# A new order of steps in batch 0 of a fused attention and feed-forward kernel, with its strided V loaded head by head

## The chip, the cores and the metric

The kernel runs on one core of a Trainium2 chip. The metric is the device time of one execution in microseconds (us); a kernel is given by the median of its runs. A core has five engines with instruction queues of their own: TensorE (PE, matmuls and the loads of their weights), VectorE (DVE), ScalarE (ACT), GpSimd (POOL) and SyncE (SP). An engine takes its queue in order, and waits on semaphores for what others make. POOL and SP also issue DMA transfers. PE writes its results to PSUM, which has eight banks; DVE and ACT read them there.

## The reference

Sparse attention over 8 batches and 8 heads of 576 positions with 64 elements each, then a feed-forward layer over all 4608 tokens:

```python
scores = scale * np.matmul(q, k.transpose(0, 1, 3, 2))
rel = pos[:, None] - pos[None, :]
mask_local = (rel >= 0) & (rel < stride)                       # heads 0 to 3, stride = 32
mask_strided = (rel >= 0) & (pos[None, :] % stride == pos[:, None] % stride)   # heads 4 to 7
scores = np.where(masks, scores, -1e9); attn = softmax(scores)
x = (attn @ v).transpose(0, 2, 1, 3).reshape(B * S, H * D)
out = (relu(x @ w_in) ** 2) @ w_out                            # 512 -> 2048 -> 512
```

## The kernel before

The feed-forward layer is done in nine chunks of 512 tokens: for each, 16 × 4 matmuls on w_in (`mm1`, line 856; `ff` is one of the 16 blocks of 128 hidden columns, `kk` one of the four blocks of 128 input rows), Relu on ACT (862), the square on DVE (866), and 16 × 4 matmuls on w_out (`mm2`, 962). The last two chunks take another way (932). The attention of batches 1 to 7 is woven between these matmuls by `PLAN`, which names for each group of four matmuls the steps that go ahead of it. Batch 0 has nothing to hide behind, since the first chunk needs its result; its steps stand in the string `BATCH0`, one word a step, and are issued in that order by `run_step`. All engines get their instructions in the order in which the steps issue them. So the order of the words is the order of the queues.

A unit is a pair of heads. Units 0 and 1 of batch 0 are local heads (0 to 3), units 2 and 3 strided ones (4 to 7). The words, with the PSUM bank that a step writes behind the slash (a step that takes a pair of banks takes this one and the next):

- `c1kv`: cast unit 1's k on the engine given by the last letter (a is ACT, v is DVE, g is POOL), line 303. `T1kv/0`: six transposes of it on PE (492) into bank 0, and a copy from there by DVE (499) into kTl; for q into qT.
- `W0k1v/5`: the same for the strided heads: transposes of half 1 of batch 0's strided k (337), and a copy (342) into kT_s; for q into qT_s. The source is staged in parts of w_out's tile, loaded by line 314.
- `b3.0/2`: the mask bias of unit 3, half 0: one matmul of the identity with a stored bias into each bank of the pair 2 and 3 (514), which starts the sums there.
- `S3.0`: the scores of unit 3, half 0, added onto that bias (544), and their exp on ACT (548). Where no `b` has gone before, `S` writes the bias itself and its word carries the bank.
- `N3/2`: sums of the exps by matmuls with ones (768), then Ln and Exp on ACT (770, 772), for a strided unit. `O3/2`: its product with V (782), and the division by the sums on DVE (784) into xt, the input of the feed-forward layer.
- `D0/4`: the product of a local unit's exps with V, which carries a column of ones (797), reciprocal and product on DVE (803, 804) into x_l. `E0v/4`: six transposes of that (837) and a copy (840) into xt.
- `H0v`: V of the local heads, shifted by 32 rows, on DVE (450). `z`: the mask of the later batches, on DVE (1067, 1068). `w1/7`: one matmul on a cleared tile (979), with no use but to keep PE at work.
- `P01/5`: the four partial sums of the first chunk's `ff` 1 begin with `kk` 0, in bank 5. Sixteen such words, for `ff` 0 to 3, end the string.

The loads that batch 0 and the first chunk need are issued ahead of the string by `load_v0` and its neighbours: q and k of unit 0 on SP, and on POOL, in this order, strided q, strided k (`load_str_rows`, 314), unit 1's q and k (296), V of the local heads (443), V of the strided heads (757), and w_in in four pieces (455). The first two pieces hold `ff` 0 to 3 (`kk` 0 and 2, then 1 and 3), the third `ff` 4 to 9, the fourth the rest. V of the strided heads goes to a part of the first chunk's tile g_sb that is free until then. It is cast from 32 to 16 bits under way, as all loads on POOL are.

Of the kernel before, what the change touches and what calls it, by code (L numbers as in the profile page):

```python
# [14 lines left out]

NP = 4
BATCH0 = """
    c0qa c0kv T0qa/2 w1/7 T0kv/5 S0.1/0 W0q0v/3 S0.0/4 W0q1v/2 b3.1/6 z W0k0a/1 W0k1v/5 b3.0/2 c1kv w1/0 S3.1
    b2.1/4 S3.0 c1qv T1kv/0 H0v S2.1 b2.0/6 S2.0 N3/2 T1qv/1 D0/4 b1.0/6 S1.0 b1.1/0 O3/2 S1.1 E0v/4 N2/6 D1/0
    P01/5 P02/3 O2/6 P03/2 P00/4 P30 P31 P32 P33 E1a/1 P20 P21 P22 P23 P10 P11 P12 P13  # L20
"""
PLAN = """
# [117 lines left out]
def kernel(  # L140
# [9 lines left out]
    nc = tc.nc  # L150
# [8 lines left out]
    NJ = 8  # L159
# [96 lines left out]
    b0 = g_pool.tile([128, 16, 512], BF16, name="g_sb").rearrange("p a c -> p (a c)")  # L256
    n_s = 4 * NJ * D
    vs0 = b0[0:SP_, 0:n_s].rearrange("p (u n d) -> p u n d", u=2, d=D)
# [181 lines left out]
    def load_v_local_sw(b):  # L440
        i = (2 * b) % NV
        t = vl_all[:, i:i + 2]
        nc.gpsimd.dma_start(out=t[32:128, :, :, :, 0:D].rearrange("p u h t d -> p (u h t) d"),  # L443
                            in_=v[b, 0:4].rearrange("h (t p) d -> p (h t) d", p=QL))
        for u in range(2):
            st.setdefault(4 * b + u, {})["v"] = t[:, u]
# [307 lines left out]

    def load_v0():
        load_v_local_sw(0)
        nc.gpsimd.dma_start(
            out=vs0.rearrange("p u n d -> p (u n d)").rearrange("p (h c) -> p h c", h=4),
            in_=v[0, 4:8].rearrange("h (p j) d -> p h (j d)", j=NJ))

    def step_N(u):
        e, hw = st[u]["e"], S // 2
# [354 lines left out]
    for i in range(2):  # L1117
# [8 lines left out]
                            NEG, -NEG, op0=ALU.mult, op1=ALU.add)  # L1126
    load_qk_local_sw(0, (1,))
    load_v0()
    for i in range(4):
        load_w_in(i)  # L1130
# [35 lines left out]
    for line in PLAN.strip().splitlines():  # L1166
        n, words = line.split(":")
# [42 lines left out]
```

## Time and profile before

| | us |
|---|---|
| median of 3 runs | 295.37 |
| lowest, highest | 295.08, 299.47 |
| the profiled execution: its time | 295.08 |
| the profiled execution: span of the core | 293.4 |

The span runs from the first instruction to the last in the profile; the profiled execution's time holds 1.7 us more around it. The mean granted clock of TensorE in it was 0.998 of full speed. Rows of groups and timelines give a start and a length in us, the engine, the line of the kernel, what is written and read, how many instructions, and in brackets the idle time of the engine ahead of them with what ended it. The chain of waits follows the last instruction back to what released it, step by step. Matmuls are pipelined: a row's length holds the time until the last result is out, and the next group begins before that, so the pace of PE is read from one start to the next. In answers by stretch the numbers are the length, then busy time and count for PE, weight loads, DVE, ACT and POOL, the granted clock, the share of the DMA engines and GB/s.

### The profile page before, as it was taken

What the parts mean: (1) busy time and instruction counts of PE and PEld (TensorE: products, weight loads), DVE (VectorE), ACT (ScalarE), POOL (GpSimd) and SP (SyncE); (2) the same over time, 40 slices, a digit from 0 to 9 for tenths busy, and PEclk for the clock granted to TensorE, in tenths of its full rate; (3) what the DMA queues carried; (4) which work ended last, traced back from release to release, by engine and by line L of the source; (5) the groups of instructions that cost most, each with busy time, mean ns of one, the idle gap of its engine ahead of it and who ended that gap; (6) DMA issues with size and microseconds to landing.
All of it is one profiled execution on the core that took longest, in us unless ns stands there. A gap on an engine that the chain in (4) does not pass through costs nothing.

```text
span 293.4 us, 6453 instructions
## 1 busy us (share of the span) xinstructions
PE 287.2 (98%) x2506; PEld 152.5 (52%) x2506; DVE 199.9 (68%) x489; ACT 167.0 (57%) x306; POOL 86.7 (30%) x135
## 2 busy tenths in 40 slices
PE   7999999999999999999999999999999999999995
PEld 3554555544444454544445444444444444984594
DVE  5666797776366746866366826673389979968983
ACT  3767846674657644764567446654676367306610
POOL 8974552062343047074303720000000013102300
PEclk9999999999999999999999999999999999999999
DMA  7999999999999999999998997411001200020003
GB/s 151 180 210 207 199 201 181 171 246 107 185 218 165 129 190 212 152 135 179 179 141 115 178 169 147 84 56 74 36 22 38 93 36 0 2 107 37 2 1 143
DMA packets 91470, 37.23 MB, mean 127 GB/s; under 512 B 77668, under 2 KB 84226, under 8 KB 91440
## 3 DMA queue, kind: packets, MB, share of 16 engines
q0 software_dynamic: 50352, 18.14, 55.6%
q1 hardware_dynamic: 40944, 18.62, 31.2%
q8 instruction: 19, 0.31, 0.4%
q14 instruction: 11, 0.09, 0.1%
q10 hardware_dynamic: 144, 0.07, 0.1%
HBM read 36.83 MB, written 9.44 MB: 158 GB/s over the span
## 4 chain that ended last, share of the span: by engine, by line
PE 96%; DMA 2%; DVE 0%; issue 0%; DVEq 0%; POOLq 0%
PE psb L856 43%; PE psb L962 33%; PE psb L932 9%; DMA w_out_b<-in_q_dram 2%; PE psb L815 2%; PE psb L589 1%; PE psb L544 1%; PE psb L492 1%; PE psb L743 1%; PE psb L680 1%; PE psb L748 1%; PE psb L514 1%; PE psb L337 0%; PE psb L837 0%; PE psb L327 0%
## 5 line engine op out<-in xcount | busy, mean ns | idle before, releaser
L856 PE MATMUL psb<-xt,w_in 128*128 128x512 bf16 x576 | 131.6, 379 | 0.0
L862 ACT ACTIVATE r<-psb 128x512 bf16<-128x512 f32 x144 | 85.6, 599 | 45.6 <-PE psb L856 42.5
L962 PE MATMUL psb<-w_out_b,g_sb 128*128 128x512 bf16 x448 | 101.0, 379 | 0.0
L856 PEld LDWEIGHTS <-w_in 128*128 128x128 bf16 x576 | 53.8, 98 | 60.3 <-issue 0.5
L866 DVE TENSOR_TENSOR g_sb<-r 128x512 bf16<-128x512 bf16 x112 | 47.0, 423 | 43.8 <-ACT r L862 42.6
L962 PEld LDWEIGHTS <-g_sb 128*128 128x128 bf16 x448 | 42.0, 98 | 47.6
L966 ACT COPY y<-psb 128x512 f32<-128x512 f32 x28 | 16.5, 589 | 42.6 <-PE psb L962 42.5
L901 POOL CAST sa<-g_sb 128x256 fp32r<-128x256 bf16 x16 | 9.7, 603 | 98.1 <-DVE g_sb L896 98.1
L725 DVE TENSOR_TENSOR xt<-psb,rv 64x288 bf16<-64x288 f32 x36 | 17.3, 479 | 14.3 <-ACT rv L713 13.9
L599 ACT ACTIVATE e<-psb 128x384 bf16<-128x384 f32 x36 | 15.5, 505 | 2.8 <-PE psb L589 2.8
L821 DVE TENSOR_TENSOR x_l<-psb,rinv 96x384 bf16<-96x384 f32 x28 | 15.5, 554 | 1.0
L596 DVE TENSOR_TENSOR e<-e,mask_all 128x576 bf16<-128x576 bf16 x24 | 10.0, 454 | 8.8 <-ACT e L599 8.6
L896 DVE TENSOR_TENSOR g_sb<-r 128x512 bf16<-128x512 bf16 x32 | 13.0, 419 | 3.3 <-ACT r L862 3.3
L355 POOL DMA_DIRECT2D q_t<-in_q_dram x6 | 3.4, 568 | 38.0 <-DMA qT_s<-q_t 35.9
L284 POOL DMA_DIRECT2D q_l<-in_q_dram x16 | 11.6, 729 | 8.1 <-DMA v_s<-in_v_dram 3.7
L284 POOL DMA_DIRECT2D k_l<-in_k_dram x16 | 11.7, 735 | 1.7 <-issue 0.9
L932 PE MATMUL psb<-t,s 128*128 128x256 f32 x96 | 12.2, 283 | 0.0
L718 DVE TENSOR_TENSOR xt<-psb,rv 64x162 bf16<-64x162 f32 x24 | 11.2, 469 | 1.2 <-ACT rv L713 0.5
L932 PEld LDWEIGHTS psb<-t,s 128*128 128x128 f32 x96 | 11.6, 189 | 0.0
L355 POOL DMA_DIRECT2D k_t<-in_k_dram x6 | 3.2, 536 | 27.3 <-DMA kT_s<-k_t 25.9
L944 DVE TENSOR_TENSOR y<-psb,y 128x256 f32<-128x256 f32 x19 | 8.0, 423 | 4.3 <-PE psb L932 3.5
L443 POOL DMA_DIRECT2D vl<-in_v_dram x8 | 9.8, 1226 | 3.8 <-DVE xt L718 2.9
(153 smaller groups left out, 303.4 us busy)
## 6 DMA issues: line engine op xcount, KB each, us to landing
out_dram<-y SPq DMA_DIRECT2D x35, 256.0 KB, 2.7
vl<-in_v_dram POOLq DMA_DIRECT2D x8, 288.0 KB, 8.2
w_out_b<-in_moe_w_out_dram POOLq DMA_DIRECT2D x4, 512.0 KB, 14.7
q_t<-in_q_dram POOLq DMA_DIRECT2D x7, 288.0 KB, 6.3
k_t<-in_k_dram POOLq DMA_DIRECT2D x7, 288.0 KB, 7.2
w_in<-in_moe_w_in_dram POOLq DMA_DIRECT2D x2, 768.0 KB, 13.5
v_s<-in_v_dram POOLq DMA_DIRECT2D x12, 108.0 KB, 7.7
k_l<-in_k_dram POOLq DMA_DIRECT2D x16, 72.0 KB, 7.5
```

Source lines behind the costliest of these rows:

```text
L284: nc.gpsimd.dma_start(out=t[:, :, hh, :], in_=src[b, 2 * p + hh].rearrange("(t p) d -> p t d", p=QL))
L599: nc.scalar.activation(e[:, row, 4 * QL * i:4 * QL * (i + 1)], bk[row][i][:, 0:4 * QL], AF.Exp, scale=scale)
L718: nc.vector.tensor_tensor(t, po[half(par), f].rearrange("c (a g m) -> c g m a", a=n, g=3), rv[half(par), w * f:w * (f + 1)].rearrange("c ( ...
L725: nc.vector.tensor_tensor(to[:, :, :, :, par], po[half(par)].rearrange("c f (a h m) -> c h m f a", a=n, h=3)[:, h], rv[half(par)].rearrang ...
L821: nc.vector.tensor_tensor(x, po[0:QL, :, 0:D], rinv[0:QL].to_broadcast([QL, NL, D]), op=ALU.mult)
L856: nc.tensor.matmul(ph, w_in_tile(kk, ff), xt[kk][:, 512 * c:512 * (c + 1)], start=(kk == order[0]), stop=(kk == order[-1]))
L862: nc.scalar.activation(r, ph, AF.Relu)
L866: later(1, lambda: nc.vector.tensor_tensor(g[:, ff, :], r, r, op=ALU.mult))
L896: nc.vector.tensor_tensor(g[:, ff, :], r, r, op=ALU.mult)
L932: nc.tensor.matmul(pa, a, b, start=k == 0 and n not in "273", stop=k == 7, skip_group_check=True)
L962: nc.tensor.matmul(py, g[:, ff, 128 * j:128 * (j + 1)], w_out_b[:, ff, :], start=(ff == 0), stop=(ff == 15))
L966: nc.scalar.copy(y, py)
```

## The change

The words of `BATCH0` are put into another order, with other banks, and one warm-up word (`w1/0`) is left out. No step is added. The biases b0.1 (which `S0.1` wrote itself) and b2.0 come before the first scores, b2.1 and b3.1 where their banks allow, `z` goes between the two copies of strided q, T1q before S2.0 and ahead of H0v, b1.0 ahead of D0, S1.0 and S1.1 ahead of O3. V of the strided heads is loaded by four transfers of 72 partitions × 512 elements instead of one of 72 × 4 × 512.

```diff
 BATCH0 = """
-    c0qa c0kv T0qa/2 w1/7 T0kv/5 S0.1/0 W0q0v/3 S0.0/4 W0q1v/2 b3.1/6 z W0k0a/1 W0k1v/5 b3.0/2 c1kv w1/0 S3.1
-    b2.1/4 S3.0 c1qv T1kv/0 H0v S2.1 b2.0/6 S2.0 N3/2 T1qv/1 D0/4 b1.0/6 S1.0 b1.1/0 O3/2 S1.1 E0v/4 N2/6 D1/0
+    c0qa c0kv T0qa/2 w1/7 T0kv/5 b0.1/0 b2.0/6 S0.1 W0q0v/3 z S0.0/4 W0q1v/2 b3.1/0 W0k0a/3 W0k1v/2 b2.1/4 S3.1
+    c1kv b3.0/2 S3.0 c1qv T1kv/0 S2.1 T1qv/1 H0v S2.0 N3/2 b1.0/6 D0/4 S1.0 b1.1/0 S1.1 O3/2 E0v/4 N2/6 D1/0
     P01/5 P02/3 O2/6 P03/2 P00/4 P30 P31 P32 P33 E1a/1 P20 P21 P22 P23 P10 P11 P12 P13
 """
...
     def load_v0():
         load_v_local_sw(0)
-        nc.gpsimd.dma_start(
-            out=vs0.rearrange("p u n d -> p (u n d)").rearrange("p (h c) -> p h c", h=4),
-            in_=v[0, 4:8].rearrange("h (p j) d -> p h (j d)", j=NJ))
+        to = vs0.rearrange("p u n d -> p (u n d)").rearrange("p (h c) -> p h c", h=4)
+        for h in range(4):
+            nc.gpsimd.dma_start(out=to[:, h], in_=v[0, 4 + h].rearrange("(p j) d -> p (j d)", j=NJ))
```

In the built program the queues of ACT and SP are in the same order as before. On PE two instructions fewer stand (the warm-up matmul and its weight load), on POOL three transfers more. The transfers that POOL issues take eight semaphores in turn, before and after.

## Prediction

> **What bounds the kernel now.** I read the page first: its busy times and the shares of the chain of work that ended last.
>
> ```profile
> PE 287.2 (98%) x2506; PEld 152.5 (52%) x2506; DVE 199.9 (68%) x489; ACT 167.0 (57%) x306; POOL 86.7 (30%) x135
> PE 96%; DMA 2%; DVE 0%; issue 0%; DVEq 0%; POOLq 0%
> ```
>
> TensorE (PE) carries the end. Second, the windows by stage (PE's share is the first number after the comma) say where it still has holes.
>
> ```profile
> 5.20:10.40 5.20, 4.21 (x61) 2.77 (x60) 2.86 (x7) 2.58 (x4) 5.20 (x7) 1.00 1.43 174
> 10.40:16.80 6.40, 6.03 (x118) 4.05 (x119) 5.36 (x10) 5.35 (x9) 6.03 (x8) 1.00 1.40 194
> 16.80:21.10 4.30, 4.30 (x45) 2.00 (x41) 1.85 (x3) 2.16 (x5) 2.99 (x4) 1.00 1.15 209
> 21.10:50.00 28.90, 28.90 (x270) 15.58 (x270) 22.29 (x59) 20.20 (x42) 13.02 (x23) 1.00 1.28 199
> ```
>
> From 16.8 to 50 us PE has no hole, and the chain leaves PE hardly room for one later, so the change, which lies wholly before 21 us, can only shift the start of that dense stretch. Even if every hole between 5.2 and 16.8 us went, 0.99 + 0.37 = 1.4 us would be won, 0.5% of the span. Two things can set the start of the dense stretch: PE's own chain through batch 0, and the third piece of w_in, which ff 4 needs. The timelines of PE and of its weight loads show both (start, length, line, what ended an idle time).
>
> ```profile
> 7.12 0.30 PE L544 MATMUL psb<-qT,kTl 64*128 64x96 bf16 x6 [0.61 <-DVE kTl L499]
> 7.79 0.43 PE L337 MATMUL psb<-ident,w_out_b 96*128 96x96 bf16 x6 [0.37 <-DMA w_out_b<-in_q_dram]
> 9.22 0.68 PE L337 MATMUL psb<-ident,w_out_b 96*128 96x96 bf16 x12
> 9.99 0.38 PE L979 MATMUL psb<-xt 128*128 128x512 bf16 x1
> 10.38 0.56 PE L544 MATMUL psb<-qT_s,kT_s 64*72 64x72 bf16 x8
> 11.49 0.43 PE L492 MATMUL psb<-ident,k_l 96*128 96x96 bf16 x6
> 11.85 0.33 PE L544 MATMUL psb<-qT_s,kT_s 64*72 64x72 bf16 x8
> 12.11 0.44 PE L514 MATMUL psb<-w_out_b,ident 72*72 72x288 bf16 x2
> 12.48 0.33 PE L544 MATMUL psb<-qT_s,kT_s 64*72 64x72 bf16 x8
> 13.10 0.43 PE L492 MATMUL psb<-ident,q_l 96*128 96x96 bf16 x6
> 13.37 0.53 PE L797 MATMUL psb<-vl,e 128*128 128x65 bf16 x12
> 14.45 0.30 PE L544 MATMUL psb<-qT,kTl 64*128 64x96 bf16 x6 [0.31 <-DVE qT L499]
> 15.65 0.43 PE L837 MATMUL psb<-ident,x_l 96*128 96x96 bf16 x6
> 16.83 0.59 PE L856 MATMUL psb<-xt,w_in 128*128 128x512 bf16 x2
> 21.11 4.86 PEld L856 LDWEIGHTS <-w_in 128*128 128x128 bf16 x24 [0.39 <-DMA w_in<-in_moe_w_in_dram]
> ```
>
> The last row is the second gate: PE's queue of weight loads reaches ff 4 and finds w_in not there. The loads beside it (issue times in POOL's timeline; KB and time from issue to landing in the answers on the DMA issues):
>
> ```profile
> 5.81 1.18 POOL L443 DMA_DIRECT2D vl<-in_v_dram  x1
> 6.98 0.75 POOL L757 DMA_DIRECT2D g_sb<-in_v_dram  x1
> 7.73 2.93 POOL L455 DMA_DIRECT2D w_in<-in_moe_w_in_dram  x4
> 13.28 0.56 POOL L318 DMA_DIRECT2D q_t<-in_q_dram  x1 [0.29 <-POOL q_t L1085]
> 25.13 0.55 POOL L430 DMA_DIRECT2D v_st<-in_v_dram  x1 [2.81 <-DMA w_in<-in_moe_w_in_dram]
> g_sb<-in_v_dram POOLq DMA_DIRECT2D x1, 288.0 KB, 7.5
> w_in<-in_moe_w_in_dram POOLq DMA_DIRECT2D x1, 256.0 KB, 8.0
> w_in<-in_moe_w_in_dram POOLq DMA_DIRECT2D x1, 768.0 KB, 11.9
> vl<-in_v_dram POOLq DMA_DIRECT2D x1, 288.0 KB, 6.8
> ```
>
> They land at 5.81 + 6.8 = 12.6 (V of the local heads), 6.98 + 7.5 = 14.5 (strided V), 7.73 + 8.0 = 15.7 (first piece of w_in) and 9.19 + 11.9 = 21.1 us (third piece). The first piece, issued 0.75 us after the strided V, lands 1.2 us after it though each takes 7.5 to 8 us: the loads queue behind each other, and the queue, not the issue, sets when they land. So PE's chain and w_in meet at 21.1 us almost exactly, and a gain needs both.
>
> **The change part by part.** *Biases ahead.* b2.0 (a two-matmul bias of scores, 12.11 to 12.48 = 0.37 us of PE) goes into the hole of 0.61 us that ended at 7.12; that hole waits for DVE's kTl copy, so it costs nothing there and takes 0.37 us out of the later stretch. b0.1 only stands before S0.1 as it did. The warm-up matmul at 9.99 goes: it stood where PE waits for ACT's kT_s copy, which ends 10.33, so nothing is won. *z moves up* between the two qT_s copies, and the rows of DVE and ACT for this and what follows are:
>
> ```profile
> 9.18 0.46 DVE L342 COPY qT_s<-psb 128x576 bf16<-128x576 bf16 x1 [0.46 <-PE psb L337]
> 9.55 0.50 DVE L1067 COPY mask_all<-mask_loc 128x576 bf16<-128x576 bf16 x1
> 10.16 0.46 DVE L342 COPY kT_s<-psb 128x576 bf16<-128x576 bf16 x1
> 11.96 0.76 DVE L499 COPY kTl<-psb 128x576 bf16<-128x576 bf16 x1 [0.45 <-PE psb L492]
> 12.75 0.58 DVE L450 COPY vl<-vl 32x1280 bf16<-32x1280 bf16 x1
> 13.64 0.76 DVE L499 COPY qT<-psb 128x576 bf16<-128x576 bf16 x1 [0.31 <-PE psb L492]
> 14.31 0.22 DVE L803 RECIPROCAL rinv<-psb 96x12 f32<-96x12 f32 x1
> 14.57 0.95 DVE L804 TENSOR_TENSOR x_l<-psb,rinv 96x768 bf16<-96x768 f32 x1
> 9.69 0.64 ACT L342 COPY kT_s<-psb 128x576 bf16<-128x576 bf16 x1 [0.29 <-PE psb L337]
> 10.98 2.51 ACT L548 ACTIVATE e<-psb 72x576 bf16<-72x576 f32 x4 [0.65 <-PE psb L544]
> ```
>
> z takes 9.55 to 10.16, 0.61 us; the idle time that it now falls into is 0.46 us and copies overlap by some 0.08, so the second qT_s copy ends about 9.72 instead of 9.64. *Banks.* W0k1 now writes bank 2, which that copy reads: it starts about 9.77, not at 9.22 + 0.68/2, some 9.5. DVE's kT_s copy, which waited for z, now waits for PE: 10.25 to 10.71 against 10.62. S3.1 starts at 10.4 as before and ends 0.08 later, at 11.02. Its exp on ACT (2.51/4 = 0.63 us each) runs 11.06 to 11.70.
>
> T1k now writes bank 0, which S3.1's scores hold until that exp has read them. By PE's own pace it would start at 11.57; it waits until 11.75, 0.26 later than the 11.49 of before. The kTl copy on DVE follows, 12.22 to 12.98 (0.76). *T1q ahead of S2.0.* T1q starts 0.26 after S2.1, at 12.37; its copy, which in the trace held S1.0 until 14.45, now runs right behind the other, to about 13.7, and S1.0 waits for it no more. What is late next: behind it on DVE stands H0v (0.58 us), which before went first. It ends about 14.25, and all of D0 but its first matmul needs the shifted V: D0 runs from 14.3 instead of 13.37. *b1.0 ahead of D0.* It writes banks 6 and 7, where S2.0's scores stand until its exp has ended: S2.0 is on PE at 12.73 to 13.06, its exp at 13.10 to 13.75, so b1.0 starts at 13.80, with D0 queued behind it; by this alone D0 would start at 14.05. Both waits lie in the same place, and H0v's ends last.
>
> From D0 the way to the dense stretch is fixed: D0's 0.5 us to 14.8, reciprocal 0.2 and x_l 0.95 to 16.1, E0 at 16.1 instead of 15.65 (+0.45). The bias, S1.0, S1.1 and O3 fit before it. E0, N2 and D1 keep their 16.83 − 15.65 = 1.18 us at most, so the first matmul on w_in is at some 17.25, +0.4. From there to ff 4 PE needs 4.2 us (4.28 in the trace, with the last 0.1 a wait for w_in, which now is in time): 21.45 against 21.11. Taken: **+0.3 us**. Bounds: if H0v ends earlier than I put it and only b1.0's wait is left, D0 at 14.05 gives +0.1; if each of the three new hand-overs (bank 2, bank 0, banks 6 and 7) costs 0.1 more, +0.6. Below nothing, too: were none of them waited for, PE would save the 0.37 of the bias and the 0.45 between S1.0's own pace (14.0) and 14.45, and the gate would be w_in. I take the value near the upper half because each wait follows from rows with less than 0.2 us of slack.
>
> *V by heads.* One issue of 0.75 us becomes four. No 72-partition issue of one head is in the trace; the nearest rows are 0.56 us (q_t, 72 partitions) and 0.75 (the load replaced), so POOL is later by 4 × 0.56 − 0.75 = 1.5 to 4 × 0.75 − 0.75 = 2.25 us. Behind stand w_in, the rest of batch 0 and 1 and w_out. The third piece of w_in would be issued at 10.7 to 11.4; the DMA queue reaches it only after the pieces before it, which land from 15.7 on. Cost nothing while that backlog of 4 us or more lasts; without it, up to 2.25 us. Each load on POOL also waits for the one eight before it (the row at 25.13: the 18th load waits for w_in's last piece, the 10th). The fourth piece of w_in thus comes to wait for the local V, landed at 12.6, instead of going out at 9.9; again before the queue gets to it. O3 needs the last V head at 15.4; the whole V landed at 14.5. Cost 0.
>
> [...]
>
> Sum: 295.08 (the profiled execution; span 293.4) + 0.3 = 295.4. The median of the runs shown, 295.37, is 0.29 above it, and that is the base of the forecast: 295.37 + 0.3 = **295.7 us**.
>
> **The rivals.** [...]
>
> *No change.* The bias taken away and the waits added cancel, and w_in still lands at 21.1: 295.4.
>
> *Slower: w_in late.* If the four V loads run one behind another, each with its own time in the queue (14.5 − 12.6 = 1.9 us for the whole V), w_in lands 3 × 1.9 = 5.7 us later, at 26.8, and the dense stretch with it: 301. It costs from the point where w_in passes 21.45, and passes 2% at 21.11 + 5.9 = 27.0. With only half of it, 298. Against: the backlog above.
>
> **How the numbers follow.** Forecast (+0.1 to +0.6) 0.55; faster 0.2; no change 0.17; slower by w_in 0.08, a quarter of it beyond 2%. 2% is 5.9 us, about what a measurement of this kernel can tell from no change; even the whole hole of 1.4 us stays within it. Hence faster 0.01, same 0.97, slower 0.02. The range runs from the lower end of the faster rival, 294.5, to the forecast's upper bound with 0.5 of the late-w_in case, 295.37 + 0.6 + 0.5 = 296.5; the likeliest case by itself is 295.4 to 296.0.
>
> **What would show it.** In the changed profile: two strided biases before 7.1 us; T1k (L492 on k_l) at 11.75 behind an ACT wait; H0v (L450) after both L499 copies and D0 (L797) ending at 14.8; E0 (L837) at 16.1, the first L856 at 17.2 to 17.3, and ff 4 at 21.4 to 21.5 with no wait for w_in. Four V issues of 0.5 to 0.75 us on POOL, w_in 1.5 to 2.3 us later issued and no later landed. Wrong if D0 starts before 14.0, or if the weight loads of ff 4 again end a wait for w_in.

## The result and the profile after

| | before | the whole change |
|---|---|---|
| runs | 22 | 22 |
| median, us | 295.18 | 296.37 |
| lowest, highest | 294.54, 299.47 | 295.15, 301.71 |
| runs at or above 298 us | 1 | 10 |
| median of the other runs | 295.16 | 295.56 |
| the profiled execution, its span | 295.08, 293.4 | 295.50, 293.8 |

The kernel became slower: the ratio after to before is 1.0058 [1.0034, 1.0081], some 1.7 us, and stays within 2%. A ratio, here and below, leaves out the runs more than 1.5% above the fastest of the same kernel (of the changed kernel those at 301.42 and 301.71 us), so where long runs are many, as in some experiments, it understates them and the counts say more.

The runs of the changed kernel fall into two groups with nothing between them. Twelve lie from 295.15 to 296.39 us, and the mean granted clock of TensorE in them was 0.992 to 1.000. Ten lie from 298.22 to 301.71, with a clock of 0.972 to 0.988. The profiled execution is of the first group. So there are two things to explain: 0.4 us between the lower groups (295.56 − 295.16), and 3 to 6 us, which some executions pay and others do not. The first is not steady: measured again twice (e5_again and f16_again below), it was 0.20 and 0.02 us.

What this execution pays for the order can be read in the profile after. First the page's busy times: PE has the warm-up matmul less, POOL the three transfers more.

```profile
PE 284.4 (97%) x2469; PEld 152.7 (52%) x2505; DVE 199.6 (68%) x489; ACT 167.0 (57%) x306; POOL 87.6 (30%) x138
```

Then the windows by stage, with the same columns as in the prediction.

```profile
5.20:10.40 5.20, 4.13 (x60) 2.64 (x58) 2.55 (x7) 2.58 (x4) 4.55 (x8) 1.00 1.24 159
10.40:16.80 6.40, 5.58 (x107) 3.83 (x108) 4.80 (x10) 4.99 (x8) 4.82 (x7) 1.00 1.44 190
16.80:21.10 4.30, 4.15 (x49) 2.27 (x50) 2.09 (x4) 2.21 (x4) 4.20 (x5) 1.00 1.15 207
21.10:50.00 28.90, 28.63 (x265) 15.46 (x269) 21.71 (x58) 20.27 (x41) 13.70 (x25) 1.00 1.29 201
```

PE's holes between 5.2 and 16.8 us have grown from 0.99 + 0.37 = 1.36 us to 1.07 + 0.82 = 1.89. The second row holds most of it. The timelines of PE, of its weight loads and of DVE show the steps that the prediction named:

```profile
6.92 0.30 PE L544 MATMUL psb<-qT,kTl 64*128 64x96 bf16 x6 [0.36 <-DVE kTl L499]
9.27 0.70 PE L337 MATMUL psb<-ident,w_out_b 96*128 96x96 bf16 x12
10.43 0.35 PE L544 MATMUL psb<-qT_s,kT_s 64*72 64x72 bf16 x8 [0.21 <-ACT kT_s L342]
11.52 0.41 PE L492 MATMUL psb<-ident,k_l 96*128 96x96 bf16 x6
12.13 0.43 PE L492 MATMUL psb<-ident,q_l 96*128 96x96 bf16 x6
13.55 0.41 PE L514 MATMUL psb<-w_out_b,ident 128*128 128x288 bf16 x2 [0.37 <-ACT e L548]
13.80 0.81 PE L797 MATMUL psb<-vl,e 128*128 128x65 bf16 x12
15.99 0.43 PE L837 MATMUL psb<-ident,x_l 96*128 96x96 bf16 x6 [0.18 <-DVE x_l L804]
17.09 0.38 PE L856 MATMUL psb<-xt,w_in 128*128 128x512 bf16 x1
21.39 0.55 PEld L856 LDWEIGHTS <-w_in 128*128 128x128 bf16 x4 [0.41 <-DMA w_in<-in_moe_w_in_dram]
12.72 0.75 DVE L499 COPY qT<-psb 128x576 bf16<-128x576 bf16 x1
13.50 0.57 DVE L450 COPY vl<-vl 32x1280 bf16<-32x1280 bf16 x1
```

H0v (L450) now stands behind both kTl and qT and ends at 14.07, so D0 (L797), which began with 0.53 us at 13.37, takes 0.81 from 13.80. E0 (L837) is 0.34 us later, the first matmul on w_in 0.26, the weight loads of ff 4 0.28. That is the 0.3 to 0.4 us of this execution. In the profiles of e5_again and f16_again the first matmul on w_in came as late (17.12 and 17.16), but the weight loads of ff 4 did not wait for w_in and came at 21.12 and 21.17, against 21.11 before. POOL's issues and the DMA answer:

```profile
6.72 2.20 POOL L759 DMA_DIRECT2D g_sb<-in_v_dram  x4
9.51 2.28 POOL L455 DMA_DIRECT2D w_in<-in_moe_w_in_dram  x3 [0.59 <-DMA w_out_b<-in_k_dram]
13.03 0.74 POOL L455 DMA_DIRECT2D w_in<-in_moe_w_in_dram  x1 [1.24 <-DMA vl<-in_v_dram]
w_in<-in_moe_w_in_dram POOLq DMA_DIRECT2D x1, 768.0 KB, 10.3
```

The issues of w_in begin 1.8 us later (9.51 against 7.73), but its third piece, issued at 11.0, takes 10.3 us where it took 11.9, and lands at 21.3 against 21.1 (at 20.9 in another profiled execution of the same kernel, e5_again below). Nothing in this profile explains the second group, since its clock was full. That needed the experiments.

### The profile page after: what moved, and what is told of

The parts are those of the page before. It is cut to its first block, busy times and chain, and to the rows that moved or that the text cites. A ratio compares the mean times of both kernels' runs of the same rounds, so it can differ in the third digit from the quotient of the medians.

```text
span 293.8 us, 6417 instructions
## 1 busy us (share of the span) xinstructions
PE 284.4 (97%) x2469; PEld 152.7 (52%) x2505; DVE 199.6 (68%) x489; ACT 167.0 (57%) x306; POOL 87.6 (30%) x138
## 4 chain that ended last, share of the span: by engine, by line
PE 88%; DVE 5%; DMA 2%; issue 2%; ACT 1%; POOL 0%; DVEq 0%; POOLq 0%
PE psb L856 38%; PE psb L962 33%; PE psb L932 9%; DMA w_out_b<-in_k_dram 2%; DVE g_sb L896 2%; PE psb L815 2%; PE psb L589 1%; DVE s L903 1%; DVE s L902 1%; PE psb L492 1%; PE psb L743 1%; PE psb L680 1%; PE psb L748 1%; PE psb L544 0%; PE psb L837 0%
## 5 line engine op out<-in xcount | busy, mean ns | idle before, releaser
L856 PE MATMUL psb<-xt,w_in 128*128 128x512 bf16 x556 | 130.1, 379 | 1.0
L962 PE MATMUL psb<-w_out_b,g_sb 128*128 128x512 bf16 x432 | 99.0, 379 | 1.4 <-issue 0.8
L856 PEld LDWEIGHTS <-w_in 128*128 128x128 bf16 x576 | 53.8, 98 | 60.3 <-DMA w_in<-in_moe_w_in_dram 0.4
L725 DVE TENSOR_TENSOR xt<-psb,rv 64x288 bf16<-64x288 f32 x36 | 17.2, 479 | 14.5 <-ACT rv L713 14.0
L718 DVE TENSOR_TENSOR xt<-psb,rv 64x162 bf16<-64x162 f32 x24 | 11.2, 467 | 1.2 <-ACT rv L713 0.5
L815 PEld LDWEIGHTS <-e 128*128 128x128 bf16 x168 | 8.2, 98 | 5.0
## 6 DMA issues: line engine op xcount, KB each, us to landing
w_in<-in_moe_w_in_dram POOLq DMA_DIRECT2D x2, 768.0 KB, 11.2
```

The source lines that it names most:

```text
L725: nc.vector.tensor_tensor(to[:, :, :, :, par], po[half(par)].rearrange("c f (a h m) -> c h m f a", a=n, h=3)[:, h], rv[half(par)].rearrang ...
L815: nc.tensor.matmul(po[:, n, :], e[:, c:c + 128], rhs[:, NL * part + n, 0:D + 1], start=True, stop=True)
L856: nc.tensor.matmul(ph, w_in_tile(kk, ff), xt[kk][:, 512 * c:512 * (c + 1)], start=(kk == order[0]), stop=(kk == order[-1]))
L962: nc.tensor.matmul(py, g[:, ff, 128 * j:128 * (j + 1)], w_out_b[:, ff, :], start=(ff == 0), stop=(ff == 15))
```

## The experiments

Three theories. **Path**: the change costs what PE's chain and w_in show, up to 0.4 us, and the rest is chance. **Clock**: the new order leaves PE emptier in batch 0, and in some executions TensorE's granted clock falls back there (0.50 in the profiles of e2_order and f14_order below). **Heads**: the four V loads cause it, by what they do to POOL and the DMA queue. In the diffs below, only the words of `BATCH0` that change and their neighbours are shown; the first line says against which kernel. The numbers are collected in this table. "High" counts the runs at or above 298 us, "long fall" those of them with a mean clock of 0.989 or less. One stretch of 3.41 us at half clock (e6_fill's profile below has one, the four others with a fall three or four) takes 0.6% off the mean of a span of 293 us, to 0.994, so a long fall is, by its mean clock, two such stretches or more. Of the 22 runs above, all ten high ones are long falls, but elsewhere seven high runs of variants lie at 0.993 or 0.994, and three, of e8_h0 and f15_d0_first, at 0.998 to 1.000: those three are long for another reason than the clock, and the 1.7 us (3.41 / 2) that one stretch costs at most is not all of what the seven pay. "Low median" is that of the runs below 298 us, with before's beside it.

| kernel | runs | high | long fall | low median, us (before) | ratio to before [95%] | before beside it: runs, high |
|---|---|---|---|---|---|---|
| whole change | 22 | 10 | 10 | 295.56 (295.16) | 1.0058 [1.0034, 1.0081] | 22, 1 |
| e5_again (the same) | 12 | 3 | 3 | 295.59 (295.39) | 1.0020 [0.9994, 1.0046] | 29, 2 |
| f16_again (the same) | 12 | 2 | 2 | 295.38 (295.36) | 1.0007 [0.9982, 1.0033] | 35, 2 |
| e1_heads | 12 | 1 | 0 | 295.34 (295.39) | 1.0014 [0.9990, 1.0039] | 35, 2 |
| e2_order | 12 | 2 | 2 | 295.27 (295.39) | 1.0010 [0.9986, 1.0034] | 35, 2 |
| f14_order (the same) | 12 | 3 | 3 | 295.18 (295.36) | 1.0021 [0.9988, 1.0055] | 35, 2 |
| e3_nowarm | 12 | 2 | 2 | 295.29 (295.39) | 1.0006 [0.9982, 1.0030] | 35, 2 |
| e4_warm | 12 | 1 | 0 | 295.73 (295.39) | 1.0014 [0.9997, 1.0031] | 35, 2 |
| e6_fill | 12 | 2 | 0 | 295.51 (295.39) | 1.0012 [0.9996, 1.0027] | 29, 2 |
| f13_fill_d0 | 12 | 1 | 0 | 295.62 (295.36) | 1.0021 [0.9996, 1.0046] | 35, 2 |
| e7_hole | 6 | 5 | 5 | 295.74 (295.39), one run | 1.0105 [1.0072, 1.0138] | 29, 2 |
| e10_hole_one | 10 | 8 | 8 | 295.44 (295.20), two runs | 1.0075 [1.0029, 1.0120] | 29, 1 |
| e11_hole_fill | 12 | 1 | 1 | 295.84 (295.20) | 1.0040 [1.0019, 1.0062] | 29, 1 |
| e12_before_hole | 8 | 6 | 6 | 295.46 (295.20), two runs | 1.0078 [1.0021, 1.0136] | 29, 1 |
| e8_h0 | 12 | 6 | 5 | 295.20 (295.39) | 1.0053 [1.0014, 1.0091] | 29, 2 |
| f15_d0_first | 12 | 4 | 1 | 295.15 (295.36) | 1.0021 [0.9987, 1.0055] | 35, 2 |
| g17_fill_k | 12 | 0 | 0 | 295.42 (295.29) | 1.0000 [0.9975, 1.0024] | 23, 1 |
| g18_hole_k | 11 | 1 | 1 | 295.55 (295.29) | 1.0026 [1.0003, 1.0049] | 23, 1 |
| e9_best | 12 | 2 | 1 | 295.45 (295.20) | 1.0015 [1.0004, 1.0027] | 29, 1 |

Kernels measured side by side on one chip share the runs of before: 173 of these in all, 9 of them high (5%). The mean clock is on record for eight of the nine, and six of these are long falls.

### Which half of the change

**V by heads alone** (against before: the `load_v0` lines of the change and nothing else).

> The kernel before with only the strided V loaded head by head. Theory A (the order of steps makes PE emptier in batch 0, which moves the start of the dense stretch by 0.4 us and in a part of the runs lowers TensorE's granted clock to some 0.98): same as before within 0.2 us, granted clock 0.998 or more in nearly every run, ff 4 starts at 20.9 to 21.1 us. Theory B (the V load is what costs): most runs 1 us or more above before, or a granted clock of 0.98 in a third or more of them.

1 of 12 high and no long fall, ratio 1.0014 [0.9990, 1.0039]. POOL issues w_in as late as in the whole change, and w_in lands no later for it, at some 20.9 us (the third issue at 11.2 and 9.7):

```profile
6.87 2.11 POOL L759 DMA_DIRECT2D g_sb<-in_v_dram  x4
9.74 2.23 POOL L455 DMA_DIRECT2D w_in<-in_moe_w_in_dram  x3 [0.76 <-DMA w_out_b<-in_k_dram]
w_in<-in_moe_w_in_dram POOLq DMA_DIRECT2D x1, 768.0 KB, 9.7
```

By itself the split neither costs nor gains; Heads falls as a cause of its own.

**The order alone** (against before: the two lines of words of the change, one V load), twice.

> The changed kernel with the strided V loaded by one transfer again, so the order of steps alone. Theory A: as the changed kernel, 0.4 us above before in the runs at a granted clock near 1 and a third to a half of the runs at a clock of 0.98 and 298 to 300 us. Theory B: as before, 295.2 us, in nearly all runs at a clock near 1.

> The order alone, with one V load, a second time. If the order alone does it: three to six of twelve runs at 298 us or more, as in the whole change here. If the four V loads are needed too: at most two again, and five or more in the whole change beside it.

2 and 3 of 12 high, all of them long falls; together 5 of 24, against 9 of 173, fewer than the third to a half that was expected. The low medians lie 0.12 and 0.18 us below before's, so a price of the order in the other runs is not seen. The ratios alone would have shown nothing, but both profiled executions happened to be high, and show what happens there. The page's row of granted clocks, in 40 slices of e2_order's 299.0 us, and then its windows:

```profile
PEclk9757999999999999999999999999999999999999
```

```profile
4.98:8.40 3.42, 2.92 (x45) 2.00 (x45) 1.88 (x4) 1.52 (x3) 3.42 (x5) 1.00 1.13 156
8.40:11.81 3.41, 2.44 (x43) 1.57 (x40) 1.73 (x5) 1.98 (x4) 3.37 (x6) 1.00 1.89 173
11.81:15.22 3.41, 2.96 (x34) 1.84 (x32) 2.84 (x3) 2.70 (x5) 2.91 (x4) 0.50 1.29 209
22.05:25.46 3.41, 3.41 (x15) 1.48 (x14) 0.43 (x1) 0.64 (x1) 0.55 (x1) 0.50 1.25 203
25.46:50.00 24.54, 24.54 (x233) 13.18 (x232) 17.16 (x45) 17.29 (x35) 11.87 (x21) 1.00 1.29 199
```

The clock is 1.00 from 4.98 to 11.81 us, 0.50 until 25.46, then 1.00 again until 50 us, and 0.9 or more in each later slice: 13.65 us at half speed, four times 3.41. f14_order, with the same words, fell back at the same place, for three times 3.41 us:

```profile
8.41:11.82 3.41, 2.70 (x47) 1.84 (x46) 1.91 (x7) 2.16 (x4) 3.28 (x5) 1.00 1.89 173
11.82:15.24 3.42, 3.30 (x44) 2.29 (x42) 2.00 (x3) 2.68 (x5) 2.70 (x4) 0.50 1.27 205
22.06:50.00 27.94, 27.67 (x255) 15.01 (x259) 18.84 (x51) 18.88 (x38) 12.31 (x23) 1.00 1.29 199
```

In both, PE was busy for 2.44 or 2.70 of the 3.41 us before the fall, and no single wait in that stretch was long. In e2_order the longest were these:

```profile
9.37 0.69 PE L337 MATMUL psb<-ident,w_out_b 96*128 96x96 bf16 x12 [0.63 <-DMA w_out_b<-in_k_dram]
10.52 0.34 PE L544 MATMUL psb<-qT_s,kT_s 64*72 64x72 bf16 x8 [0.23 <-ACT kT_s L342]
```

So in these two executions the price is paid inside batch 0 and the first chunk, by a lower clock. The mean clocks of the whole change's high runs fit: seven of the ten lie at 0.980 to 0.982, which is what three such stretches at half speed take out of 292 us (3 × 3.41 / 2 = 5.1 us, 1.8%).

In these windows the granted clock is 1.00 or 0.50, and each fall lasts a whole number of stretches of 3.41 us. No stretch ahead of a fall was idle (PE was busy for 2.44 and 2.70 us), and one busy stretch did not bring the clock back: it took four and three, and in both a stretch with PE busy for all of its 3.41 us (18.64 to 22.05 in e2_order, 15.24 to 18.65 in f14_order) was followed by another at half.

**Before without the second warm-up matmul.**

```diff
before
- c1kv w1/0 S3.1
+ c1kv S3.1
```

> The kernel before without its second warm-up matmul (the word w1/0 ahead of S3.1) and nothing else. Theory A1 (that matmul keeps PE busy enough for the clock): times at a clock near 1 stay within 0.1 us, but a third or more of the runs have a granted clock of 0.98 and 298 us or more. Theory A2 (the new waits of PE at 11.5, 13.2 and 14 us do it, not that matmul) and theory B: as before in nearly every run.

2 of 12 high, ratio 1.0006 [0.9982, 1.0030]. Too few to tell from before's 9 of 173; whether the removed matmul has a share stays open.

### Filling PE's holes, and widening one

The words `w2` and `w3` stand for two and three warm-up matmuls.

```diff
after -> e4_warm
- W0k1v/2 b2.1/4
+ W0k1v/2 w1/4 b2.1/4
after -> e6_fill
- W0k0a/3 W0k1v/2 b2.1/4 ... N3/2 b1.0/6 D0/4
+ w2/3 W0k0a/3 W0k1v/2 w1/4 b2.1/4 ... N3/2 w2/4 b1.0/6 w1/4 D0/4
after -> f13_fill_d0
- N3/2 b1.0/6 D0/4
+ N3/2 w1/4 b1.0/6 w1/4 D0/4
```

> The changed kernel with a warm-up matmul put back ahead of b2.1, in the place where PE waits for kT_s. Theory A1: the runs at a clock of 0.98 are gone or fall to one in ten, and the median to 295.6 us. Theory A2: a third to a half of the runs stay at 0.98 and the median 296 us or more. Theory B: no difference from the changed kernel.

> The changed kernel with six warm-up matmuls (0.22 us each) put into the holes in which PE waits: two ahead of W0k0, one ahead of b2.1, two ahead of b1.0 and one ahead of D0. Theory A: hardly any run at 298 us or more (at most one in twelve), and the rest at the changed kernel's time within 0.2 us, since the holes take them. Theory C: the share is the same as the changed kernel's here.

> The changed kernel with two warm-up matmuls in the waits of b1.0 and D0 only. If the hole at 13.2 to 14.1 us is what lets the clock be halved: at most two of twelve runs at 298 us or more, the others at the changed kernel's 295.3 to 296 us. If the hole at 9 to 10.4 us is: a third or more, as in the changed kernel.

Warm-up matmuls whose results nobody reads: 1, 2 and 1 of 12 high, together 4 of 36, where the kernel without them had 15 of 46 over its three measurements. By the clock it is plainer: the four lie at 0.993 and 0.994, so none of the 36 is a long fall, and all of the 15 are. Each filled another hole or all. Filling is no cure for all: e6_fill's profiled execution was high. PE waited 1.08 us for a cast of k that came late and worked for 1.98 of 3.42 us; the clock was 0.50 for one stretch after it:

```profile
9.28:12.69 3.41, 3.19 (x29) 2.45 (x30) 1.15 (x5) 1.35 (x3) 2.23 (x3) 0.50 1.84 166
```

The counter-test makes a hole wider with the same steps (e12_before_hole writes the mask twice). `z` (the mask copy on DVE, 0.5 us) moves ahead of H0v, so that D0 waits longer:

```diff
after -> e7_hole (e10_hole_one: the same with one V load)
- W0q0v/3 z S0.0/4 ... T1qv/1 H0v S2.0
+ W0q0v/3 S0.0/4 ... T1qv/1 z H0v S2.0
e7_hole -> e11_hole_fill
- N3/2 b1.0/6 D0/4
+ N3/2 w1/4 b1.0/6 w3/4 D0/4
before -> e12_before_hole
- b3.1/6 z W0k0a/1 ... T1kv/0 H0v
+ b3.1/6 W0k0a/1 ... T1kv/0 z z H0v
```

> The changed kernel with z (0.55 us of DVE) moved behind T1q's copy, ahead of H0v, so that PE stands about 0.5 us longer ahead of D0. Theory A: more than half of the runs at 298 us or more, and the rest at 0.5 us above the changed kernel. Theory C: the same small share; the rest 0.5 us above. If H0v is not what ends the hole ahead of D0, the rest stay at the changed kernel's time.

> The changed order with z moved ahead of H0v (PE stands longer ahead of D0) and the strided V loaded by one transfer. Theory A (an emptier PE lets TensorE's clock be halved): as with the four V loads, more than half of the runs at 298 us or more. Theory D (the order and the four V loads are both needed): one in six or fewer.

> The changed kernel with z moved ahead of H0v, and four warm-up matmuls (one ahead of b1.0, three ahead of D0) put into the hole that this makes. The steps of batch 0 end as late as without them, so ff 4 starts at 21.4 to 21.5 us. Theory A: the share of runs at 298 us or more falls from five in six to that of the changed kernel (a third) or below, and the median to 296 us or less. If the lateness of the steps and not the emptiness of PE brings those runs, the share stays above half.

> The kernel before, its own order and one V load, with z moved ahead of H0v and done twice, so that PE stands some 1 us ahead of D0. Theory A: a third or more of the runs at 298 us or more, against some one in seventeen of the kernel before, and the others 0.6 to 1 us above it. Theory D, and any theory by which it takes the new order or the new loads: one in ten or fewer at 298 us or more.

5 of 6, 8 of 10 and 6 of 8 high, all long falls: 19 of 24. With the same lateness and the hole filled, 1 of 12. e12_before_hole has the old order and one V load, so neither the new order nor the heads are needed. Its windows, and those of e10_hole_one:

```profile
11.61:15.02 3.41, 1.51 (x29) 0.88 (x24) 3.21 (x6) 2.65 (x5) 3.04 (x4) 1.00 1.20 196
15.02:25.26 10.24, 9.40 (x95) 5.28 (x96) 5.43 (x9) 2.63 (x4) 6.00 (x8) 0.50 1.19 207
25.26:50.00 24.74, 24.53 (x230) 13.26 (x232) 17.15 (x45) 17.77 (x36) 12.15 (x21) 1.00 1.31 198
```

```profile
10.14:13.55 3.41, 2.90 (x53) 1.89 (x51) 2.41 (x5) 2.84 (x5) 2.73 (x5) 1.00 1.61 180
13.55:16.96 3.41, 1.95 (x21) 1.34 (x21) 2.35 (x6) 1.47 (x4) 3.37 (x4) 0.50 1.19 197
20.37:23.79 3.42, 3.06 (x23) 1.28 (x22) 1.94 (x3) 0.64 (x1) 0.71 (x1) 0.50 1.19 208
23.79:50.00 26.21, 26.00 (x241) 14.06 (x244) 17.94 (x47) 18.15 (x36) 12.32 (x22) 1.00 1.31 199
```

In the filled kernel PE is busy where the wait was (its D0 group by the timeline):

```profile
13.15 0.39 PE L979 MATMUL psb<-xt 128*128 128x512 bf16 x1
14.05 0.59 PE L979 MATMUL psb<-xt 128*128 128x512 bf16 x2
14.48 0.53 PE L797 MATMUL psb<-vl,e 128*128 128x65 bf16 x12
```

This is the case's cleanest pair: e7_hole and e11_hole_fill differ in four warm-up matmuls alone and reach ff 4 at 21.47 and 21.50 us in their profiles, both of full clock (0.999 and 1.000), yet 5 of 6 against 1 of 12 fall back. They were measured on two chips; but e10_hole_one and e12_before_hole, with 8 of 10 and 6 of 8, ran beside the same 29 runs of before as e11_hole_fill. Clock is shown for these kernels: it is the emptiness of PE, not the lateness, that makes long falls frequent (19 of 24 against 1 of 12).

How the wider hole does it is not shown. In e12_before_hole most of the wait lies ahead of the fall, but in e10_hole_one the clock fell at 13.55, and D0's wait, 1.25 us that end at 15.70, began after that, so it did not start that fall:

```profile
15.70 0.77 PE L797 MATMUL psb<-vl,e 128*128 128x65 bf16 x11 [1.25 <-DVE vl L450]
```

### Which hole of the change itself

The change has two: the one from 9 to 10.4 us (PE waits for strided k and its copies), and D0's. Taking D0's away:

```diff
after -> e8_h0
- T1kv/0 S2.1 T1qv/1 H0v S2.0
+ T1kv/0 S2.1 H0v T1qv/1 S2.0
e8_h0 -> f15_d0_first
- N3/2 b1.0/6 D0/4
+ N3/2 D0/4 b1.0/6
f15_d0_first -> g17_fill_k (the first hole filled)
- W0k0a/3 W0k1v/2 b2.1/4
+ w2/3 W0k0a/3 W0k1v/2 w1/4 b2.1/4
f15_d0_first -> g18_hole_k (the first hole widened)
- W0q0v/3 z S0.0/4
+ W0q0v/3 z z S0.0/4
```

> The changed kernel with H0v ahead of T1q's copy on DVE again, one part of the change undone. My step that H0v sets D0: D0's second matmul moves from 14.1 to 13.8 (then the wait of b1.0 for S2.0's exp is last), ff 4 is at 21.1 to 21.2 if T1q's copy does not take its place, and the runs at full clock 0.1 to 0.2 us faster than the changed kernel. Theory A: share of runs at 298 us or more falls only a little, since the hole is 0.3 us shorter.

> The changed kernel with D0 ahead of b1.0 and H0v ahead of T1q's copy, as in the kernel before, so that neither wait stands ahead of D0. D0 starts at 13.3 to 13.5 us and ff 4 at 20.9 to 21.1 us, where w_in lands: the runs at full clock are 0.3 us faster than the changed kernel's. If the hole at 13.2 to 14.1 us is what lets the clock be halved: at most two of twelve runs at 298 us or more; if the other: a third or more.

> The changed kernel with D0 ahead of b1.0 and H0v ahead of T1q's copy (no second hole), and three warm-up matmuls in the first hole, two ahead of W0k0 and one ahead of b2.1. If the first hole is the cause: at most one of twelve runs at 298 us or more, the others at 295 to 295.4 us since ff 4 then waits for w_in at 21 us. If not: three or more, as without the three matmuls (4 of 12).

> The same without the warm-up matmuls, but with z done twice ahead of the second qT_s copy, which W0k1 waits for, so that the first hole is some 0.5 us wider. If the first hole is the cause: half or more of the runs at 298 us or more, and a profile with a halved clock has it from the end of a window that holds 9 to 10.5 us. If not: a third, as without it. The runs at full clock: 0.2 to 0.5 us above the kernel before.

Moving H0v (e8_h0) does not yet take D0's hole away. b1.0 still waits for S2.0's exp ahead of D0, which starts at 14.00 instead of 13.37:

```profile
13.76 0.40 PE L514 MATMUL psb<-w_out_b,ident 128*128 128x288 bf16 x2 [0.37 <-ACT e L548]
14.00 0.53 PE L797 MATMUL psb<-vl,e 128*128 128x65 bf16 x12
```

f15_d0_first has D0 at 13.09, ahead of b1.0. By time the two have 6 and 4 of 12 high, and by time the first hole would be the cause. The clocks say otherwise: five of e8_h0's six are long falls (0.981 to 0.983), but only one of f15_d0_first's four; the others lie at 0.994, 0.998 and 1.000. Counted by long falls, the kernels that keep D0's hole have 15 of 46 (whole change), 5 of 24 (order alone) and 5 of 12 (e8_h0). Those in which it is gone or filled have 1 of 12 (f15_d0_first), 0 of 12 (g17_fill_k), 1 of 11 (g18_hole_k) and 0 of 12 (f13_fill_d0). That points to D0's hole. The first hole, filled in g17_fill_k and widened in g18_hole_k, made no difference beside f15_d0_first, and that half or more of g18_hole_k's runs would be high was a miss. It was a weak test too, since the second `z` shows in its profile as waits of PE of only 0.2 + 0.2 us.

Two things stand against D0's hole alone. e4_warm fills the first hole and keeps D0's, with the same wait of 0.37 us for the exp, and had no long fall in 12. And both order-alone executions fell back at 11.8 us, before D0's wait and right after the stretch that holds the first hole. Which hole of the change is the one, or whether it takes both, is not settled.

### The same kernel again, and a better order

> The changed kernel once more, beside the three below and the kernel before on one chip. Theory A (its emptier PE between 8 and 16 us lets TensorE's clock be halved again for some windows in a part of the runs): a third to a half of the runs at 298 us or more, the rest 0.2 to 0.5 us above before. Theory C (the share of such runs belongs to the chip or the hour, not to the kernel): the same small share as before has here, one in ten or fewer, and a median 0.3 us above before.

> The changed kernel once more, on the same chip as the three others of this call: a third of the runs at 298 us or more, the others 0.2 to 0.5 us above the kernel before. Were it one in ten here, the share would hang on the chip or the hour more than on the kernel, and the other three could not be read.

3 and 2 of 12 high, where the first measurement had 10 of 22 and a third was expected. The low medians, 295.59 and 295.38, lie only 0.20 and 0.02 us above before's beside them. The share varies from one measurement to the next, with the program the same; over all three it is 15 of 46 against before's 9 of 173. The order alone had 5 of 24; so few runs cannot tell 5 of 24 from 15 of 46, so whether the four V loads add to the share stays open.

e9_best is a version meant to beat both kernels, with one V load:

```diff
after -> e9_best (and banks of later words given out anew)
- b2.1/4 S3.1 ... T1kv/0 S2.1 T1qv/1 H0v S2.0 N3/2 b1.0/6 D0/4
+ w1/4 S3.1 ... T1kv/4 b2.1/0 S2.1 H0v T1qv/5 S2.0 N3/2 D0/0 b1.0/6
```

> An order of my own: b2.0 ahead and a warm-up matmul as in the changed kernel with it put back, but b2.1 and T1k in banks that are free (T1k no longer waits for the exp of S3.1), H0v ahead of T1q's copy, D0 ahead of b1.0 in a pair of its own, and one V load. By my two gates: PE reaches ff 4 before w_in is there, at 20.9 to 21.1 us with a wait for w_in, so the time is the kernel before's within 0.2 us and no better; at most one run in eight at 298 us or more, since PE's holes are as short as in the kernel before. If the chain through batch 0 alone sets the start, 0.3 us or more faster.

Ratio 1.0015 [1.0004, 1.0027]: not better than before. Its profiled execution (296.29 us) has ff 4 as soon as w_in lets it, 0.4 us earlier than before, but lost 1.4 us at 115 us to a wait for another transfer:

```profile
20.74 1.19 PEld L856 LDWEIGHTS <-w_in 128*128 128x128 bf16 x7 [0.49 <-DMA w_in<-in_moe_w_in_dram]
```

```profile
PE psb L856 <- DMA xt<-x_l: 1.4, 1, 1.4
```

By the ratios none of the variants beats before; g17_fill_k comes nearest, at 1.0000 [0.9975, 1.0024].

## Why the prediction was wrong

It gave 295.7 us for a kernel that stays at full clock, and that is where those runs lie: 295.56. The median is 296.37, because almost half of the first 22 runs were not at full clock. How far it is off hangs on their share, which is partly luck: in the two repeats the medians (295.88 and 295.49) lie 0.48 and 0.12 us above before's, on both sides of the forecast 0.3.

- **The failed step: a hole of PE was priced at its length.** "Even if every hole between 5.2 and 16.8 us went, 0.99 + 0.37 = 1.4 us would be won", it says, and the new waits were added up as 0.1 to 0.6 us. The runs show a second price: in the profiles, stretches with waits of 0.63 us (the longest ahead of the fall in e2_order) to 2.4 us (D0's in e12_before_hole) were followed by three or four stretches of 3.41 us at half clock, and runs with such a clock are 3 to 6 us longer. A wider hole made them 19 of 24, the same hole filled 1 of 12. No rival held this, although the kernel before had warm-up words in the string ("no use but to keep PE at work") and a run at 299.47.
- **The warm-up matmul: "nothing is won".** Its time was indeed covered, but its other use was not weighed. Whether its loss matters is open (e3_nowarm); that added ones help is shown (no long fall in 36, against 15 in 46).
- **b2.0 ahead: right.** S0.1 starts at 6.92 after a wait of 0.36, and the bias is gone from the later stretch.
- **Bank 0: right, but 0.2 us earlier.** T1k started at 11.52, not 11.75, as soon as the exp of S3.1 had ended (11.47); S3.1's scores took 0.35 us where the prediction kept the 0.56 of before and added 0.08. **Banks 6 and 7: right**, b1.0 waits 0.37 us for the exp and starts 13.55 (forecast 13.80).
- **H0v, D0, E0, first L856: right** in cause and within 0.25 us: H0v ends 14.07 (14.25), D0's group ends 14.61 (14.8), E0 15.99 (16.1), L856 17.09 (17.2 to 17.3). All are 0.1 to 0.2 us earlier than forecast, as T1k was. D0's first matmul, at 13.80, came before the 14.0 that was to show the account wrong; the second, which needs H0v, came at 14.12.
- **ff 4 "with no wait for w_in": wrong in this execution.** It came at 21.39 behind 0.41 us of waiting for w_in. In e5_again and f16_again, with the same program, no such wait ended there. Both gates lie within 0.3 us of each other. In these two ff 4 came 4.00 and 4.01 us after the first L856 (17.12 to 21.12 and 17.16 to 21.17), so the 4.2 us of the sum was 0.2 too much: the 4.28 of before held more of the wait for w_in than the 0.1 taken out.
- **V by heads at nothing: right**, by e1_heads. POOL's delay of 1.8 us lies in the forecast 1.5 to 2.25, though by luck: the four issues took 1.45 us more (2.20 against 0.75), and 0.59 us went to a wait for the strided k that was not in the sum, with POOL some 0.26 us earlier at the start. w_in's fourth piece waited for the local V as said (1.24 us), and the backlog hid it. The lower end of the range, 294.5, has w_in land 0.6 us sooner. No run shows this term: w_in landed at 21.3 in the changed kernel, at 20.9 in e1_heads, and with one V load at 21.1 in the kernel before and at 20.9 in e3_nowarm.

Left open: what makes the clock fall, and what brings it back. Stretches with 2.44 (e2_order) and even 2.90 us of PE work (e10_hole_one) were followed by half clock, but ones with 2.43 (before) and 2.45 (e7_hole) were not:

```profile
5.59:9.00 3.41, 2.43 (x40) 1.60 (x38) 1.31 (x3) 1.54 (x3) 3.41 (x5) 1.00 1.21 177
```

```profile
13.27:16.68 3.41, 2.45 (x50) 1.70 (x50) 2.63 (x7) 2.75 (x5) 3.04 (x6) 1.00 1.21 207
```

The stretches are counted in steps of 3.41 us from where the clock of that execution first rose to full (5.59 us in the kernel before). PE's busy share by itself does not separate the two kinds. Nor does it tell when the clock comes back: after a first stretch at half clock with PE busy for 3.19 us (e6_fill) it did, after one with 3.30 (f14_order) it did not. The whole change itself was profiled three times, each time at full clock: that its high runs fall back in the same stretch of the kernel as the order alone is inferred from their mean clocks and from the variants, not seen.

## What to carry to other kernels

In this kernel a hole in TensorE's work before the first dense stretch had two prices: its length, and the chance that the clock was halved around or after it (0.50 for 3.41 to 13.65 us in the five profiles with a fall; long falls in 19 of 24 runs with a hole made wider, in 1 of 12 with it filled). Look for the second in the spread of the runs and in the mean clock of each, since a profile of a good run does not show it (1.000 in all three of the whole change), and not every long run has a low clock (three from 298.02 to 298.68 us lie at 0.998 to 1.000). Where a reorder opens such a hole, fill it with idle matmuls of the same length and count the runs with a low clock: a pair like e7_hole and e11_hole_fill, equally late but one empty and one filled, tells clock from lateness. A kernel whose runs fall into two groups is not described by a median, and two measurements of a dozen runs can differ by the share alone.

## What the hardware showed beyond this

In the five profiles with a fall the clock fell back for whole stretches of 3.41 us: three in e10_hole_one, e12_before_hole and f14_order, four in e2_order, one in e6_fill. The three of e12_before_hole passed although PE was busy for 9.40 of their 10.24 us.

H0v took 0.57 us in the changed kernel's profile and 0.48 in e11_hole_fill's, but 1.57 in e10_hole_one's, 1.53 in e2_order's and 1.63 in e12_before_hole's. In e10_hole_one and e2_order it began just after a memset on POOL (14.07 after 14.04, 13.89 after 13.80). In e10_hole_one, DVE and then POOL:

```profile
14.07 1.57 DVE L450 COPY vl<-vl 32x1280 bf16<-32x1280 bf16 x1
```

```profile
14.04 1.27 POOL L1088 MEMSET vb<- 128x1408 f32 x1
```

The copy ends at 15.64, 0.33 us after the memset's end at 15.31. f14_order shows the other order: there H0v came first and kept its 0.48 us, and the memset took 1.58 instead of 1.27. In these rows the one that began second took longer; why it did is not shown.

```profile
13.97 0.48 DVE L450 COPY vl<-vl 32x1280 bf16<-32x1280 bf16 x1
14.09 1.58 POOL L1088 MEMSET vb<- 128x1408 f32 x1
```

With four V loads POOL comes to that memset at 17.00 and the two do not meet: so D0's hole is wider in e10_hole_one and e12_before_hole than the order of their words tells.
